# Gaps of 160 and 224 bytes between the weight tiles in on-chip memory

## The chip, the cores and the metric

One core of one Trainium2 chip runs the whole kernel. The metric is the device time of one execution in microseconds (us); the time before is the median of three runs.

## The reference

Eight sequences of 3,072 vectors of 256 floats pass through three layers, all in float32:

```python
X = np.fft.fft(np.fft.fft(x, axis=1), axis=2).real        # 8 x 3072 x 256
x = X.reshape(24576, 256)
# mixture of 8 experts, the best one only
logits = normalised(x) @ normalised(expert_emb).T / tau
e = argmax(logits); gate = softmax(logits)[e]
x = gate * (relu(x @ w1[e]) @ w2[e])                       # w1: 256x1024, w2: 1024x256
# dense layer
h = x @ w_in                                               # 256x2048
out = maximum(0.01 * h, h) @ w_out                         # 2048x256
```

## The kernel before

**Layers.** `batch` computes the two Fourier transforms of one sequence as matmuls with small tables (`smat`, lines 339 to 345, and `cols`, line 453), writes the rows to memory and lets `route` choose each token's expert and write its number into that expert's list. `main` then works through pages of 256 tokens of one expert. A page's rows are gathered, turned by TensorE (`split_t`, line 931) and passed through the expert (`m1_a`, line 947, then `m1_b`, line 965) and the dense layer (`m2_a`, line 1020, then `m2_b`, lines 1056 to 1060). Pages that no expert fills are done in halves by `m3_a` (line 979) and `m3_b` (line 992).

**Precision.** Each float32 operand of these layers is held as a sum of a high and a low part, and a product is made of three matmuls: high by high, high by low, low by high (`PASS`). Both operands have the type float32r.

**A matmul's two operands.** TensorE first loads the stationary operand, 128 columns, and then streams the other one through. In the profile the first is LDWEIGHTS (PEld) and the second MATMUL (PE). In `m1_a`, `m1_b` and `m2_a` the weights `w1`, `w2` and `wi` are stationary and the tokens `xt`, `hh` and `yt` are streamed, 256 columns at a time. In `m2_b` it is the other way: the tokens `hh` are stationary and the weights `wo` are streamed, 512 columns (line 1059, both parts of the weights) and then 256 (line 1060). In `m3_a` and `m3_b`, too, the weights are streamed. Every matmul has a load of its own.

**Memory.** Tiles lie one behind the other in each partition, pool by pool, in the order in which they are first made. The pool `cp` (tables and constants) is first, then `xp`, which begins with the four weight tiles, and last `mp`, which holds `xt`, `yt` and `hh`. `mp` takes the place of `ip`, a pool of the start. The tiles of `mp` are 4,096 bytes a partition each, and `wi`, `wo`, `w1` and `w2` are 32,768, 32,768, 16,384 and 16,384 bytes; within all of these a matmul's operand begins at a multiple of 512 bytes from the tile's start. So the place of an operand modulo 256 is that of its tile.

**Order of the work.** A list of steps written out by `main` sets the order on TensorE: each step issues 12 to 24 matmuls of a first layer (`m1_a`, `m2_a`) and, three steps later, those of the second (`m1_b`, `m2_b`), while `side` mixes in the next sequence's Fourier transform.

Of the kernel before, what the change touches and what calls it, by code (L numbers as in the profile page):

```python
# [6 lines left out]
F32 = mybir.dt.float32  # L7
# [25 lines left out]
BIG = 1e9  # L33
NTB = 3
C3 = 0.8660254037844386
LAG = 3
AHEAD = 13
GAP = 1
# [25 lines left out]
class K:  # L64
# [9 lines left out]
    def run(self):  # L74
        nc, V, a, tc = self.nc, self.V, self.a, self.tc
        dram = self.pool("dram", 1, bass.MemoryType.DRAM)
        self.xd = dram.tile([NTOK, D], F32, name="xd")
        self.tables = [dram.tile([E * NTOK + T, 4], F32, name=f"table{i}") for i in range(NTB)]
        self.bigd = dram.tile([128, 768], F32, name="bigd")
        self.yd = dram.tile([REST + T, D], F32, name="yd")  # L80
        self.dt = dram.tile([REST + T, 4], F32, name="dt")
        self.leftd = dram.tile([NB * 8, 2, 6, 16], F32, name="leftd")
        cp = self.pool("cp", 1)
        self.psm = self.pool("psm", 1, bass.MemoryType.PSUM)
        self.xp = self.pool("xp", 1)
        self.wi = self.xp.tile([128, 2, 2, F2], F32R, name="wi")
        self.wo = self.xp.tile([128, 2, 16, D], F32R, name="wo")
        self.w1 = self.xp.tile([128, 2, 2, F1], F32R, name="w1")
        self.w2 = self.xp.tile([128, 2, 8, D], F32R, name="w2")
        self.wide, self.turn = True, 0  # L90
        with tc.manual_schedule():
            self.consts(cp)
            self.main()

    def ps(self, tag, shape, bufs):
        return self.psm.tile(shape, F32, tag=tag, name=tag, bufs=bufs)
# [132 lines left out]
    def column_end(self, ip):  # L229
# [10 lines left out]
        for d0, n, s0 in ((4, 2, 0), (8, 2, 2)):  # L240
            V.scalar_tensor_tensor(zp[:, d0:d0 + n], zy[:, 10 + s0:10 + s0 + n], -C3, zy[:, 5 + s0:5 + s0 + n], op0=ALU.mult, op1=ALU.add)
            yield
        for d0, n, s0 in ((6, 1, 4), (7, 1, 1), (10, 2, 2)):
            V.scalar_tensor_tensor(zp[:, d0:d0 + n], zy[:, 10 + s0:10 + s0 + n], C3, zy[:, 5 + s0:5 + s0 + n], op0=ALU.mult, op1=ALU.add)
            yield
# [102 lines left out]
    def s_stage(self, j, f, gd, z, left, ptmp):  # L348
# [13 lines left out]
        for par, (sa, sb) in enumerate(r1):  # L362
# [7 lines left out]
            o = 513 + 512 * par  # L370
            V.scalar_tensor_tensor(z[:, o:o + 256], p[:, l:l + 256], -C3 if j == 0 else C3, tmp[:, l:l + 256], op0=ALU.mult, op1=ALU.add)
            if par == 0:
                pv, tv = (x[:, 0:258].rearrange("p (a b) -> p a b", a=2)[:, :, 0:128] for x in (p, tmp))
                V.scalar_tensor_tensor(z[:, 769:1025].rearrange("p (a b) -> p a b", a=2), pv, C3, tv, op0=ALU.mult, op1=op)
            else:
                V.scalar_tensor_tensor(z[:, 1281:1537], p[:, 0:256], C3, tmp[:, 0:256], op0=ALU.mult, op1=op)
            yield "s"
# [386 lines left out]
    def decodes(self):  # L764
# [41 lines left out]
        def rolling(i, end):  # L806

            run = [unit(i)]
            i += 1
            n = 0  # L810
            while run:
                for g in list(run):
                    if next(g, "end") == "end":
                        run.remove(g)
                        if i < end:
                            run.append(unit(i))
                            i += 1
                            next(run[-1])
                    yield
                    n += 1  # L820
                    if n == SKEW and i < end:
                        run.append(unit(i))
                        i += 1
# [11 lines left out]
    def main(self):  # L835
# [53 lines left out]
        def load_page(u):  # L889
            n = 2 if u < NFULL else 1  # L890
            off = nc.sync.value_load(self.rg[:, 0, u:u + 1], min_val=0, max_val=ZPAGE * 2 // n)
            t3 = self.xp.tile([128, NTB, 8], F32, tag="t3", name="t3", bufs=2)
            for i, tb in enumerate(self.tables):
                nc.sync.dma_start(out=t3[:, i, 0:4 * n], in_=tb[bass.ds(off * (H * n), H * n)].rearrange("(p h) w -> p (h w)", h=n))
            t3s[u] = t3[:, :, 0:4 * n]
# [45 lines left out]
        def m1_a(u, s, fill):  # L941
            p = self.ps("h", [128, 2, T], 3)
            xt = xts[u]
            for f in range(2):
                fc = 2 * s + f
                for k, (dc, (wa, xa)) in enumerate([(dc, ps_) for dc in range(2) for ps_ in PASS]):
                    nc.tensor.matmul(p[:, f], self.w1[:, wa, dc, fc * 128:(fc + 1) * 128], xt[:, xa, dc], start=(k == 0), stop=(k == 5))  # L947
            h = self.mp.tile([128, 2, 2, T], F32R, tag="hh", name="hh", bufs=LAG + 1)
            nc.scalar.activation(h[:, 0], p, AF.Relu)  # L949
# [78 lines left out]
        def split_g():  # L1028

            if owed:  # L1030
                m, u, s, g = owed.pop()
                h = self.mp.tile([128, 2, 2, T], F32R, tag="hh", name="hh", bufs=LAG + 1)
                if m == 3:
# [44 lines left out]
        def at(i, fn, *args):  # L1078
            hooks.setdefault(max(0, i), []).append((fn, args))
# [4 lines left out]
        for n, (i, u) in enumerate(firsts):  # L1084
# [5 lines left out]
            if n:  # L1090
# [4 lines left out]
                s0, s1 = end, min(end + 1, i)  # L1095
                s2, s3 = max(pos[pm, pu, na // 2 - 1] + LAG + 2, s0 + 2), max(min(end + LAG, i + LAG), s1 + 2)
                at(max(ip_ + 1, ls[0]), wload, u, 0)
# [10 lines left out]
        for t in range(NTF):  # L1108
            i = [k for k, s in enumerate(steps) if s == (2, NU + t, 0)][0]
# [11 lines left out]
        with tc.tile_pool(name="ip", bufs=1) as self.ip:  # L1121
# [34 lines left out]
            fetch_page(0)  # L1156
            load_page(1)
        self.mp = self.pool("mp", 1)
        self.wide = False
        for _ in range(FIRST[2]):  # L1160
            next(dec)
# [36 lines left out]
        def lag(n):  # L1198

            return 1 if steps[n] in ((1, 0, 3), (1, 1, 3)) else LAG if n > SHORT else 2  # L1200

        done = 0
        for i in range(len(steps) + LAG):
            for fn, args in hooks.get(i, ()):
# [161 lines left out]
```

## Time and profile before

| | |
|---|---|
| three runs | 3680.07, 3681.48, 3687.99 us; median 3681.48 us |
| the profiled execution | 3645.73 us, its span 3644.0 us |
| TensorE, mean granted clock | 0.985 |
| matmuls (MATMUL records) | 26,433 |
| TensorE busy / loading | 97% / 92% of the span |
| VectorE, ScalarE, GpSimd busy | 66%, 53%, 18% |

The span runs from the first to the last instruction of the profiled execution, and 1.7 us of that execution lie outside it. The busy share of TensorE says how long a matmul was under way, not how fast the columns ran: matmuls overlap, so the time of a stretch comes from the distance between their starts.

### The profile page before, as it was taken

How to read it: one execution, taken by the hardware profiler on the slowest of the kernel's cores; microseconds unless marked ns; L12 is line 12 of the kernel's file. 1: busy time of each engine (PE TensorE's matmuls, PEld its weight loads, DVE VectorE, ACT ScalarE, POOL GpSimd, SP SyncE). 2: the span in 40 equal slices, each digit the busy share in tenths (PEclk: the TensorE clock that was granted, in tenths of full speed). 3: DMA queues.
4: the chain of work that ended last, by engine and by line, in shares of the span. 5: the costliest groups of instructions: out<-in, count | busy, mean ns of one | idle time of the engine just before them, and what ended most of it. 6: DMA issues, size and time to landing. Idle time of an engine off the chain costs nothing. (4 is left out here: it accounts for less than half of the span.)

```text
span 3644.0 us, 69226 instructions
## 1 busy us (share of the span) xinstructions
PE 3517.8 (97%) x26433; PEld 3352.5 (92%) x26433; DVE 2413.9 (66%) x4783; ACT 1919.5 (53%) x3475; POOL 671.2 (18%) x620
## 2 busy tenths in 40 slices
PE   4598999999999999999999999999999999999998
PEld 3588999999999999999999999999999999999998
DVE  8776766666666766667666675667676567777654
ACT  3354446554655446554565446554555456666543
POOL 2214111411122111411114111231114111111100
PEclk8799999999999999999999999999999999999999
DMA  4432323332323322332233323232233245555300
GB/s 159 138 122 91 103 65 104 87 133 64 109 71 113 97 72 95 86 116 82 80 99 89 124 71 95 87 104 92 80 100 88 76 124 159 152 154 153 103 24 15
DMA packets 266145, 362.22 MB, mean 99 GB/s; under 512 B 75984, under 2 KB 216659, under 8 KB 265620
## 3 DMA queue, kind: packets, MB, share of 16 engines
q1 hardware_dynamic: 238896, 303.66, 27.6%
q0 software_dynamic: 25184, 52.35, 4.4%
q8 instruction: 207, 3.39, 0.4%
q10 hardware_dynamic: 1732, 1.79, 0.2%
q14 instruction: 126, 1.03, 0.1%
HBM read 304.64 MB, written 63.41 MB: 101 GB/s over the span
## 5 line engine op out<-in xcount | busy, mean ns | idle before, releaser
L1020 PE MATMUL h<-yt,wi 128*128 128x256 f32 x9216 | 1216.6, 281 | 1.1 <-DVE yt L970 1.1
L1020 PEld LDWEIGHTS h<-yt,wi 128*128 128x128 f32 x9216 | 1135.8, 189 | 14.5 <-DVE yt L970 1.3
L1059 PE MATMUL o<-wo,hh 128*128 128x512 f32 x3008 | 1104.1, 400 | 6.9 <-DVE ob L1070 6.9
L1022 ACT ACTIVATE g<-h 128x512 f32<-128x512 f32 x768 | 457.4, 596 | 788.0 <-PE h L1020 782.6
L1060 PE MATMUL o<-wo,hh 128*128 128x256 f32 x3008 | 844.5, 281 | 0.0
L1023 DVE TENSOR_TENSOR g<-g,h 128x512 f32<-128x512 f32 x768 | 525.5, 684 | 451.7 <-ACT g L1022 449.1
L1059 PEld LDWEIGHTS o<-wo,hh 128*128 128x128 f32 x3008 | 566.1, 188 | 109.6 <-DVE ob L1070 7.1
L925 DVE TENSOR_TENSOR w<-raw,w 128x1024 fp32r<-128x1024 f32 x440 | 536.7, 1223 | 148.6 <-ACT w L924 145.6
L1071 POOL DMA_INDIRECT out<-ob,tab x192 | 208.4, 1085 | 2268.6 <-DVE ob L1070 1982.3
L1060 PEld LDWEIGHTS o<-wo,hh 128*128 128x128 f32 x3008 | 568.7, 189 | 1.6
L965 PE MATMUL y<-hh,w 128*128 128x256 f32 x4272 | 566.1, 282 | 1.9 <-DVE w L925 1.3
L947 PE MATMUL h<-xt,w 128*128 128x256 f32 x4224 | 557.4, 282 | 4.6 <-ACT xt L933 3.6
L950 DVE SCALAR_TENSOR_TENSOR hh<-h,hh 128x512 fp32r<-128x512 f32 x356 | 245.9, 691 | 453.9 <-ACT hh L949 453.9
L947 PEld LDWEIGHTS h<-xt,w 128*128 128x128 f32 x4224 | 524.5, 190 | 19.6 <-ACT xt L933 4.3
L965 PEld LDWEIGHTS y<-hh,w 128*128 128x128 f32 x4272 | 528.7, 189 | 3.0 <-DVE w L925 1.5
L1040 DVE TENSOR_TENSOR hh<-g,hh 128x512 fp32r<-128x512 f32 x768 | 525.7, 684 | 1.5 <-ACT hh L1039 1.4
L924 ACT ACTIVATE w<-raw 128x1024 fp32r<-128x1024 f32 x440 | 462.2, 1055 | 94.1 <-DMA raw<-w 93.2
L949 ACT ACTIVATE hh<-h 128x512 fp32r<-128x512 f32 x356 | 213.0, 598 | 551.9 <-PE h L947 550.7
L1039 ACT ACTIVATE hh<-g 128x512 fp32r<-128x512 f32 x768 | 479.0, 624 | 13.1 <-DVE g L1023 12.5
L902 POOL DMA_INDIRECT xr<-xd,tab x199 | 247.3, 1243 | 501.6 <-issue 295.3
L608 POOL DMA_INDIRECT table<-tb,sli x192 | 208.3, 1085 | 192.2 <-DVE tb L602 58.1
L931 PE MATMUL a<-ident,xr 128*128 128x128 f32 x426 | 66.0, 274 | 43.0 <-DMA xr<-xd,tab 43.0
(301 smaller groups left out, 2050.2 us busy)
## 6 DMA issues: line engine op xcount, KB each, us to landing
raw<-w SPq DMA_DIRECT2D x440, 512.0 KB
x<-xl SPq DMA_DIRECT2D x32, 768.0 KB
xd<-xo SPq DMA_DIRECT2D x96, 256.0 KB
table<-bigd SPq DMA_DIRECT2D x21, 384.0 KB
t<-table SPq DMA_DIRECT2D x267, 4.0 KB
xr<-xd,tab POOLq DMA_INDIRECT x199, 4.8
table<-tb,sli POOLq DMA_INDIRECT x192, 3.3
rawz<-w_out SPq DMA_DIRECT2D x6, 512.0 KB
```

The source lines that it names most:

```text
L902: nc.gpsimd.indirect_dma_start(out=self.xr[seq[u] % NX][:, h], out_offset=None, in_=self.xd[0:rows, :], in_offset=bass.IndirectOffsetOnAxi ...
L924: nc.scalar.activation(hi, r, AF.Copy)
L925: V.tensor_tensor(lo, r, hi.bitcast(F32), op=ALU.subtract)
L947: nc.tensor.matmul(p[:, f], self.w1[:, wa, dc, fc * 128:(fc + 1) * 128], xt[:, xa, dc], start=(k == 0), stop=(k == 5))
L965: nc.tensor.matmul(y[:, x], self.w2[:, wa, fc, xs_], h[:, ha, f], **st)
L1020: nc.tensor.matmul(p[:, f], self.wi[:, wa, dc, fc * 128:(fc + 1) * 128], yt[:, xa, dc], start=(k == 0), stop=(k == 5))
L1022: nc.scalar.activation(g, p, AF.Copy, scale=0.01)
L1023: V.tensor_tensor(g, g, p, op=ALU.max)
L1039: nc.scalar.activation(h[:, 0], g, AF.Copy)
L1040: V.tensor_tensor(h[:, 1], g, h[:, 0].bitcast(F32), op=ALU.subtract)
L1059: nc.tensor.matmul(o[th], h[:, 0, f, tk], self.wo[:, :, fc], start=(fc == 0), stop=False, skip_group_check=True)
L1060: nc.tensor.matmul(o[th][:, 0], h[:, 1, f, tk], self.wo[:, 0, fc], start=False, stop=(fc == 15), skip_group_check=True)
```

## The change

Five entries `GAPS` in bytes, and a helper that takes a tile of that size from a pool and never uses it. A gap of 224 bytes is put ahead of `wi`, one of 160 ahead of `wo`, none ahead of `w1`, one of 224 ahead of `w2`, and one of 160 at the head of `mp`.

```diff
+GAPS = 224, 160, 0, 224, 160
...
         self.xp = self.pool("xp", 1)
+        self.hole(self.xp, 0)
         self.wi = self.xp.tile([128, 2, 2, F2], F32R, name="wi")
+        self.hole(self.xp, 1)
         self.wo = self.xp.tile([128, 2, 16, D], F32R, name="wo")
+        self.hole(self.xp, 2)
         self.w1 = self.xp.tile([128, 2, 2, F1], F32R, name="w1")
+        self.hole(self.xp, 3)
         self.w2 = self.xp.tile([128, 2, 8, D], F32R, name="w2")
...
+    def hole(self, pool, i):
+
+        if GAPS[i]:
+            pool.tile([128, GAPS[i] // 4], F32, name=f"hole{i}")
...
         self.mp = self.pool("mp", 1)
+        self.hole(self.mp, 4)
```

`wi` moves by 224 bytes, `wo` and `w1` by 384, `w2` and all later tiles of `xp` by 608, and the tiles of `mp` by 768, which is three times 256. In words of the change, the streamed operand's address less the stationary one's becomes 160 (`m1_a`), 192 (`m1_b`) and 64 (`m2_a`) modulo 256, and 96 in `m2_b`. No instruction is added, removed or moved.

## Rows read from the trace of the kernel before

**Rows 1.** The page: span, and TensorE's busy time, share, instructions.

```profile
span 3644.0 us, 69226 instructions
...
PE 3517.8 (97%) x26433; PEld 3352.5 (92%) x26433; DVE 2413.9 (66%) x4783; ACT 1919.5 (53%) x3475; POOL 671.2 (18%) x620
```

**Rows 2.** Windows, core 0: two of seven stretches, us and (instructions).

```profile
core 0: us, PE busy (x) PEld busy (x) DVE busy (x) ACT busy (x) POOL busy (x), PEclk, DMA share, GB/s
...
0.00:141.00 141.00, 51.51 (x280) 47.13 (x280) 106.38 (x376) 47.41 (x120) 39.81 (x65) 0.73 0.47 152
...
1000.00:2000.00 1000.00, 1000.00 (x7631) 956.90 (x7631) 658.03 (x1285) 527.79 (x947) 207.95 (x184) 1.00 0.30 92
```

**Rows 3.** Waits of TensorE, 400 to 3600 us: all there are.

```profile
PE a L585 <- DVE ohb L577: 1.2, 1, 1.2
```

**Rows 4.** Groups by line, TensorE, whole span: count, busy us, mean ns.

```profile
L1020 PE MATMUL h<-yt,wi 128*128 128x256 f32 x9216 | 1216.6, 281 | 1.1 <-DVE yt L970 1.1
L1059 PE MATMUL o<-wo,hh 128*128 128x512 f32 x3008 | 1104.1, 400 | 6.9 <-DVE ob L1070 6.9
L1060 PE MATMUL o<-wo,hh 128*128 128x256 f32 x3008 | 844.5, 281 | 0.0
L965 PE MATMUL y<-hh,w 128*128 128x256 f32 x4272 | 566.1, 282 | 1.9 <-DVE w L925 1.3 <-ACT w L924 0.6
L947 PE MATMUL h<-xt,w 128*128 128x256 f32 x4224 | 557.4, 282 | 4.6 <-ACT xt L933 3.6 <-DVE xt L934 0.8
```

**Rows 5.** Timeline of TensorE from 2004.6 us: start, length, count.

```profile
2004.69 0.40 PE L1059 MATMUL o<-wo,hh 128*128 128x512 f32 x1
2004.92 0.28 PE L1060 MATMUL o<-wo,hh 128*128 128x256 f32 x1
...
2006.09 1.57 PE L947 MATMUL h<-xt,w 128*128 128x256 f32 x12
2007.50 0.39 PE L1059 MATMUL o<-wo,hh 128*128 128x512 f32 x1
```

**Rows 6.** Timeline of TensorE from 329 us, in a stretch at half clock.

```profile
333.98 0.63 PE L1059 MATMUL o<-wo,hh 128*128 128x512 f32 x1
...
335.89 2.34 PE L1020 MATMUL h<-yt,wi 128*128 128x256 f32 x10
```

**Rows 7.** Windows: that stretch, with the granted clock (PEclk).

```profile
329.00:338.50 9.50, 5.33 (x21) 4.95 (x22) 3.67 (x9) 0.63 (x1) 3.36 (x3) 0.50 0.59 196
```

**Rows 8.** Timeline from 2002.5 us, TensorE and its loads.

```profile
2002.81 0.28 PE L1060 MATMUL o<-wo,hh 128*128 128x256 f32 x1
2002.81 0.19 PEld L1059 LDWEIGHTS o<-wo,hh 128*128 128x128 f32 x1
```

**Rows 9.** Timeline from 173.0 us: a matmul behind which no load follows.

```profile
173.98 0.40 PE L1056 MATMUL o<-wo,hh 128*128 128x256 f32 x2
...
174.92 1.25 PEld L1056 LDWEIGHTS o<-wo,hh 128*128 128x128 f32 x10 [0.75 <-DVE hh L1040]
```

**Rows 10.** Groups in windows of 0.08 us, each holding one such matmul.

```profile
L1056 PE MATMUL o<-wo,hh 128*128 128x256 f32 x1 | 0.3, 280 | 0.0
...
L1056 PE MATMUL o<-wo,hh 128*128 128x256 f32 x1 | 0.3, 282 | 0.0
...
L1056 PE MATMUL o<-wo,hh 128*128 128x256 f32 x1 | 0.3, 277 | 0.0
```

**Rows 11.** By tile, 400 to 3600 us: duration ns minimum/median/maximum.

```profile
L1020 PE MATMUL h<-yt,wi x8523: 273/280/370, 399.8 to 3599.4; 128*128 128x256 f32 x199
...
L1059 PE MATMUL o<-wo,hh x2842: 389/393/586, 400.2 to 3599.8; 128*128 128x512 f32 x190
L1060 PE MATMUL o<-wo,hh x2841: 275/281/287, 400.4 to 3599.7; 128*128 128x256 f32 x190
```

**Rows 12.** Groups in windows of 0.025 us at 1993.9 and 1856.1 us.

```profile
L1059 PE MATMUL o<-wo,hh 128*128 128x512 f32 x1 | 0.4, 403 | 0.0
...
L1059 PE MATMUL o<-wo,hh 128*128 128x512 f32 x1 | 0.4, 393 | 0.0
```

## The prediction, made before the result was known

> **What bounds the kernel now.** I read the page first, then the windows by stage, the waits of TensorE, its groups by line, and last the timeline, where the distance between starts can be read. On the page TensorE is busy for 97% of the span [rows 1]. The windows say where the other 3% lie: in the first 141 us TensorE is busy for 51.51 us, while from 1000 to 2000 us it is never idle [rows 2]. From 400 to 3600 us it waits once, for 1.2 us [rows 3]. So no engine, queue or transfer sets the time of these 3,200 us; only how fast matmul follows matmul does. Anything that makes one matmul in this stream a nanosecond longer or shorter is paid at once, some 20,700 times for those of 256 columns (9,216 + 3,008 + 4,272 + 4,224) and 3,008 times for those of 512 [rows 4]. The other 2,705 of the 26,433 records, a tenth of them [rows 1], I leave out.
>
> The timeline gives the rate. Twelve matmuls of line 947 take from 2006.09 to 2007.50 us, 117.5 ns each, and four pairs of lines 1059 and 1060 from 2004.69 to 2006.09 us, 350 ns a pair [rows 5]. [...]
>
> [...]
>
> **The change part by part.** The gaps add no instruction, transfer or wait; the 768 bytes a partition cost nothing in time. What they move is worked out from the tile sizes. `mp` moves by 768 bytes, so `xt`, `yt` and `hh` keep their place modulo 256. `wi` moves by 224, `w1` and `wo` by 384 (128 modulo 256), `w2` by 608 (96). Taking these shifts back out of the change's own numbers gives the relation before: 64 + 224, 160 + 128 and 192 + 96 are all 288, or 32 modulo 256, for `m2_a`, `m1_a` and `m1_b`; and 96 - 128 is -32, or 224, for `m2_b`. So all stages now have the two operands within 32 bytes of each other modulo 256, and the change takes them 64 to 96 bytes apart. The other tiles of `xp` move too: the Fourier stage's operands by 96 modulo 256 and the transfers' targets with them. That costs nothing here: its matmuls are among the tenth left out, and the transfers land under a TensorE that waits 1.2 us in all [rows 3]; if that cover were gone, the wait would be seen on TensorE by line 947 or 965.
>
> Does the relation matter? A load starts at the moment at which the stream before it does: line 1060 streams and line 1059 loads from 2002.81 us on [rows 8]. So both read at once, and a clash between them is possible. [...]
>
> *From below.* Some matmuls of the start are followed by no load, because the next operand isn't ready: the second of the two of line 1056 at 173.98 us has the next load at 174.92 us [rows 9]. Such ones take 280, 282 and 277 ns; the eight that I read have a mean of 280.0, and three of them are shown [rows 10]. The median with a load beside is 280 (line 1020) and 281 (line 1060) [rows 11]. So a load beside costs a 256-column stream 0 to 1 ns, and most of its excess stays when there is nothing to clash with: 1 ns x 20,720 = 21 us at the most.
>
> *From above.* The same matmul of line 1059, the third of its step and with operands in the same tiles, takes 403 ns in one page and 393 in another [rows 12]. Its addresses are the same both times, so I put the difference down to the moment at which stream and load meet. How they meet is worth up to 10 ns of a 512-column stream. The median is 393 [rows 11], so most meet well; if all did badly it would be 10 x 3,008 = 30 us more. The pairs of rows 5 take 350 ns where 393 and 281 would make 347; I take 4 ns for the mean, 12 us.
>
> The widest bounds are the extremes of the groups: 275 and 287 ns against 281, and 389 against 393 [rows 11]. If every matmul reached its group's best, it would be 6 x 20,720 + 4 x 3,008 = 124 + 12 = 136 us less.
>
> [...]
>
> I take 21 + 12 = 33 us off: two operands that start together within 32 bytes modulo 256 are the relation at which they would most often want the same place, and the change leaves it in all four stages. That sign is an argument from the layout; no row shows another relation in these stages, and the rows bound the size alone.
>
> **The sum.** 3645.7 - 33 = 3612.7 us against the profiled execution, which was 35.8 us faster than the median of the runs. None of the steps touches that distance, so it is carried over: 3681.5 - 33 = 3648 us, 0.9% faster. A measurement here can tell 0.2%, some 7 us, from no change.
>
> **The rivals.**
>
> *Nothing happens (25%).* Load and stream do not meet, as the eight lone matmuls say, and the excess is the stream's own. Against it: the two lengths of one matmul. Time: 3681 us, within 0.2%. [...]
>
> *Slower (20%).* The relation sets the phase in which load and stream lock, and the new one is worse. The place is `m2_b`, with its two lengths: every 512-column stream at 403 ns is 30 us more. If the 256-column ones lose 1 ns as well, 21 us: 3681.5 + 51 = 3733 us. It decides from the point at which a 256-column stream's mean rises by 0.4 ns (8 us), since that alone is past 0.2%. For it: the kernel's median is already at the better length of 393, so there is more to lose there than to win.
>
> *Much faster (10%).* The excess is mostly a clash after all, and a matmul nears its group's best: 136 us less, 3545 us. Against it: the lone matmuls. [...]
>
> **How the numbers follow.** The forecast, 3648 us, has 45%; its own range goes from 8 us less, where it ends in no change, to 70 us less, twice the sum: 3611 to 3673 us. Faster: 45 + 10 = 55%; the same: 25%; slower: 20%. The range for 8 in 10 goes down to the middle of what lies between 70 and 136 us less, 103 us, 3578 us, and so leaves out half of the much faster case, 5%. Upwards it goes to 3715 us, two thirds of the way to the slower rival's price, and I leave out some 12% there.
>
> **What the profile after would show.** If the steps are right, waits and counts stay as they are, TensorE is as busy, and the median of lines 947, 965 and 1020 falls by about 1 ns, with the distance between their starts at 116 to 117 ns; the pair of lines 1059 and 1060 comes to 345 or 346 ns, and 403 becomes rare. If nothing happens, all these stay to the nanosecond. If line 1059's median goes to 400 or more, the slower rival is right. The forecast fails if a stage's relation is worse than the present one while others gain, or if the excess was a clash that the lone matmuls hide, for instance one with their own load.

## The result, and the profile after

The changed kernel took 3637.01 us (median of 3 runs, 3635.68 to 3646.85) against 3681.48 us: 44.5 us less, a ratio of 0.9895 with a 95% interval of [0.9874, 0.9917]. Six more runs against 25 of the kernel before gave 3637.3 against 3671.2 us, 0.9908 [0.9891, 0.9924]: 34 us less. This second pair is the better measured.

The two first profiles don't show that gain. Their executions took 3645.73 us before and 3646.85 us after: the one before was 36 us below its kernel's median, the one after the longest of its kernel's three runs. The page after, span and busy times, against [rows 1]:

```profile
span 3645.1 us, 69226 instructions
...
PE 3512.2 (96%) x26433; PEld 3338.5 (92%) x26433; DVE 2413.7 (66%) x4783; ACT 1917.7 (53%) x3475; POOL 690.2 (19%) x620
```

The counts are those of before. The windows after, two stretches, against [rows 2]:

```profile
0.00:141.00 141.00, 52.51 (x280) 47.92 (x280) 106.52 (x376) 47.45 (x120) 40.31 (x65) 0.73 0.47 152
1000.00:2000.00 1000.00, 1000.00 (x7669) 955.35 (x7669) 660.81 (x1289) 528.50 (x951) 216.73 (x184) 1.00 0.30 92
```

In the same 1000 us, never idle in either kernel, TensorE now begins 7669 matmuls instead of 7631, 0.5% more. Over the 3,200 us from 400 to 3600 that would be 0.5% x 3200 = 16 us, a first estimate of the gain in the streams' rate; the count over the same matmuls below gives 13. Where it lies is seen in the durations by tile after, 400 to 3600 us (minimum/median/maximum ns), against [rows 11]:

```profile
L1030 PE MATMUL h<-yt,wi x8531: 276/278/562, 399.8 to 3600.0; 128*128 128x256 f32 x199
L957 PE MATMUL h<-xt,w x3936: 277/281/287, 404.5 to 3417.4; 128*128 128x256 f32 x197
L975 PE MATMUL y<-hh,w x3936: 276/276/470, 414.4 to 3427.3; 128*128 128x256 f32 x197
...
L1069 PE MATMUL o<-wo,hh x2844: 388/394/628, 400.3 to 3598.5; 128*128 128x512 f32 x190
L1070 PE MATMUL o<-wo,hh x2844: 275/279/415, 400.5 to 3598.7; 128*128 128x256 f32 x190
```

Line numbers are ten higher. The two lines of before that [rows 11] leave out:

```profile
L947 PE MATMUL h<-xt,w x3936: 273/281/288, 401.6 to 3415.2; 128*128 128x256 f32 x197
L965 PE MATMUL y<-hh,w x3936: 275/280/469, 411.4 to 3425.3; 128*128 128x256 f32 x197
```

Line 975 (`w2`) lost 4 ns of its median and line 1030 (`wi`) 2; line 957 (`w1`) stands still, and the 512-column line 1069 has 1 ns more. The timeline after shows the rate by the starts, as [rows 5] do:

```profile
2016.64 1.52 PE L975 MATMUL y<-hh,w 128*128 128x256 f32 x12
2018.00 1.52 PE L1030 MATMUL h<-yt,wi 128*128 128x256 f32 x12
2019.36 1.52 PE L975 MATMUL y<-hh,w 128*128 128x256 f32 x12
2020.72 1.52 PE L1030 MATMUL h<-yt,wi 128*128 128x256 f32 x12
2022.08 0.40 PE L1069 MATMUL o<-wo,hh 128*128 128x512 f32 x1
...
2023.49 0.75 PE L1030 MATMUL h<-yt,wi 128*128 128x256 f32 x5
```

The same two lines in turn, in the kernel before:

```profile
2015.93 1.56 PE L965 MATMUL y<-hh,w 128*128 128x256 f32 x12
2017.33 1.56 PE L1020 MATMUL h<-yt,wi 128*128 128x256 f32 x12
2018.73 1.45 PE L965 MATMUL y<-hh,w 128*128 128x256 f32 x11
```

Twelve matmuls of lines 975 and 1030 take 1.36 us here, 113.3 ns each, where before took 1.40 us, 116.7 ns; not all steps of these lines are so quick, as the experiments show. The four pairs of lines 1069 and 1070 take 1.41 us, 352.5 ns a pair, where before took 350. The waits after, 400 to 3600 us, against the single row of [rows 3]:

```profile
PE h L1030 <- issue: 4.5, 6, 1.0
PE a L595 <- DVE ohb L587: 1.5, 1, 1.5
PE o L1070 <- issue: 0.7, 1, 0.7
PE h L1030 <- remote: 0.4, 1, 0.4
PE o L1069 <- issue: 0.4, 1, 0.4
```

"Issue" means that TensorE waited for nothing that the profile shows and yet began no matmul. Before's first profile has none of it. So the two first profiles hide the gain: a quicker stream here, and stalls of a kind that the execution before happened not to have.

### The profile page after: what moved, and what is told of

The parts are those of the page before. It is cut to its first block, busy times and chain, and to the rows that moved or that the text cites. A ratio compares the mean times of both kernels' runs of the same rounds, so it can differ in the third digit from the quotient of the medians.

```text
span 3645.1 us, 69226 instructions
## 1 busy us (share of the span) xinstructions
PE 3512.2 (96%) x26433; PEld 3338.5 (92%) x26433; DVE 2413.7 (66%) x4783; ACT 1917.7 (53%) x3475; POOL 690.2 (19%) x620
## 5 line engine op out<-in xcount | busy, mean ns | idle before, releaser
L975 PE MATMUL y<-hh,w 128*128 128x256 f32 x4272 | 555.7, 279 | 2.0 <-DVE w L935 1.3
L975 PEld LDWEIGHTS y<-hh,w 128*128 128x128 f32 x4272 | 518.9, 189 | 3.0 <-DVE w L935 1.5
L912 POOL DMA_INDIRECT xr<-xd,tab x199 | 258.4, 1299 | 508.2 <-issue 297.7
```

The source lines that it names most:

```text
L912: nc.gpsimd.indirect_dma_start(out=self.xr[seq[u] % NX][:, h], out_offset=None, in_=self.xd[0:rows, :], in_offset=bass.IndirectOffsetOnAxi ...
L975: nc.tensor.matmul(y[:, x], self.w2[:, wa, fc, xs_], h[:, ha, f], **st)
```

## The experiments

A short name for what is varied: the relation of a stage is its streamed less its stationary address modulo 256. Taking it modulo 256 is the change's own choice: in d3_wo and d2_m1 the tokens move by 256 and 512 bytes against `wi`, and the mean distance of that stage's starts is 118.3 and 118.5 ns where c0_before has 118.6. The kernel before has 32 for `wi`, `w1` and `w2` and 224 for `wo`; the changed kernel has 64, 160, 192 and 96. Two experiments run the kernels as they are, two leave out transfers, and all others change only the list `GAPS` of the changed kernel.

**Both kernels again**, without an edit.

> The kernel before, unchanged, beside itself. If the 44 us between the medians come from the change, this gives 3680 us again and a profile of 3680 us, whose stretches would show where the 35 us lie that the first profiled execution (3645.7 us) lacked. If they come from the execution (some executions of one kernel near 3646 us, some near 3681 us), this kernel's times spread over both.

> The changed kernel, unchanged. Theory of the relation: the starts of lines 1030 and 975 stay 114 ns apart in the median (117 before), which is worth 13 us from 400 to 3600 us in the two traces, so the ratio to before is 0.996 to 0.997 when both run on one chip in turn. If the 44 us are the change's, the ratio is 0.988 to 0.990.

The kernel before gave 3671.62 us, 0.9998 [0.9984, 1.0013]; the changed one 3637.3 us, 0.9908. This time the profiled executions are typical: 3669.6 and 3637.1 us. The waits of TensorE, 400 to 3600 us, kernel before:

```profile
PE h L1020 <- issue: 5.7, 11, 0.8
PE o L1059 <- issue: 4.0, 7, 0.9
PE a L585 <- DVE ohb L577: 1.2, 1, 1.2
...
```

and changed kernel:

```profile
PE a L595 <- DVE ohb L587: 1.5, 1, 1.5
PE o L1070 <- issue: 0.2, 1, 0.2
```

The timeline of the kernel before, second profile, shows what these stalls look like and what GpSimd does meanwhile:

```profile
683.69 0.98 POOL L608 DMA_INDIRECT table<-tb,sli  x1 [0.30 <-issue]
...
684.49 0.35 PE L1020 MATMUL h<-yt,wi 128*128 128x256 f32 x1 [0.28 <-issue]
...
684.97 0.98 POOL L608 DMA_INDIRECT table<-tb,sli  x1 [0.30 <-issue]
...
685.92 0.40 PE L1059 MATMUL o<-wo,hh 128*128 128x512 f32 x1 [0.72 <-issue]
...
686.63 0.39 PE L1059 MATMUL o<-wo,hh 128*128 128x512 f32 x1 [0.20 <-issue]
687.34 0.38 PE L1060 MATMUL o<-wo,hh 128*128 128x256 f32 x1 [0.31 <-issue]
688.05 0.39 PE L1059 MATMUL o<-wo,hh 128*128 128x512 f32 x1 [0.34 <-issue]
```

The slowest of these matmuls come 0.71 us apart instead of 0.12 to 0.23, while line 608 issues its indirect transfers one behind the other. The load on the DMA engines is not the reason, as the window of this stall shows (its last three numbers: granted clock, busy share of the DMA engines, GB/s):

```profile
684.00:690.00 6.00, 3.66 (x18) 2.42 (x17) 2.49 (x3) 2.66 (x4) 4.78 (x5) 1.00 0.03 2
```

In the other four stalls of this trace, too, the DMA engines are busy for 3 to 4% at 2 to 3 GB/s. Next, four stretches of 30 us, the same in both kernels, with the count of matmuls in the first brackets of a row and the granted clock behind the last ones. Kernel before, second profile:

```profile
670.00:700.00 30.00, 26.90 (x178) 24.52 (x177) 15.73 (x23) 12.87 (x20) 17.77 (x17) 0.89 0.33 89
1110.00:1140.00 30.00, 28.70 (x212) 27.14 (x212) 16.30 (x25) 13.84 (x24) 14.40 (x13) 1.00 0.35 82
1540.00:1570.00 30.00, 28.02 (x201) 26.07 (x201) 15.64 (x24) 12.90 (x22) 12.77 (x13) 1.00 0.30 64
1970.00:2000.00 30.00, 27.10 (x184) 25.02 (x184) 14.04 (x21) 12.06 (x20) 11.57 (x12) 0.94 0.22 62
```

Changed kernel, second profile:

```profile
670.00:700.00 30.00, 30.00 (x234) 28.76 (x233) 18.44 (x29) 15.73 (x25) 18.41 (x17) 1.00 0.34 90
1110.00:1140.00 30.00, 30.00 (x235) 28.84 (x234) 16.07 (x26) 13.46 (x23) 14.69 (x14) 1.00 0.37 87
1540.00:1570.00 30.00, 30.00 (x232) 28.76 (x231) 18.17 (x28) 15.39 (x25) 10.14 (x10) 1.00 0.46 110
1970.00:2000.00 30.00, 30.00 (x232) 28.71 (x231) 18.41 (x29) 15.98 (x26) 8.12 (x8) 1.00 0.44 117
```

Matmuls: 178 + 212 + 201 + 184 = 775 against 933. At the changed kernel's 120 / 933 us each, the 158 missing ones are some 20 us (roughly, since the mix of lines differs). In the first and the last of these stretches the granted clock also stood below full speed, at 0.89 and 0.94 on the mean: after 13 matmuls in the 4 us from 686 us it stood at 0.54 in the next 4 us, and after 11 in the 4 us from 1,976 us at 0.57, so partly near the 0.50 of [rows 7]. Part of what a stall costs is the slower clock: at 0.50 a pair of lines 1059 and 1060 took 637 ns [rows 6, 7], at 1.00 it took 350 [rows 5].

So the 34 us have two parts. The table gives both for every kernel. Rates are the mean distance in ns from one start to the next, 400 to 3600 us, distances of 320 ns and more left out; "pair" is a 512- and a 256-column matmul of the output weights; "stalled" is what steps took beyond the median of like steps, summed from 400 us on over those that exceed it by more than 6% plus 60 ns. Some 8 us of it are in every kernel, the stall-free ones too. All kernels issue the same matmuls in the same order, so "stretch" times the same 24,180 of them in each profile, those from 400 to 3600 us in the first profile of before. A ratio is to the kernel before run beside it.

| kernel | relation wi, w1, w2, wo | wi | w1 | w2 | pair | stalled us | stretch us | median us | ratio |
|---|---|---|---|---|---|---|---|---|---|
| before, first profile | 32, 32, 32, 224 | 118.3 | 117.5 | 118.0 | 352.5 | 7.9 | 3200.0 | 3681.48 | |
| c0_before | 32, 32, 32, 224 | 118.6 | 117.5 | 118.0 | 352.9 | 29.1 | 3221.1 | 3671.62 | 0.9998 |
| c1_after | 64, 160, 192, 96 | 116.7 | 118.2 | 115.9 | 354.2 | 9.3 | 3187.1 | 3637.3 | 0.9908 |
| c2_all96 | 32, 32, 32, 224 | 118.7 | 117.6 | 118.7 | 352.8 | 25.1 | 3222.9 | 3672.59 | 1.0012 |
| c3_mp96 | 128 in all | 120.1 | 118.6 | 119.8 | 351.3 | 19.3 | 3232.8 | 3685.58 | 1.0045 |
| d4_zero | 0 in all | 120.9 | 119.8 | 121.2 | 354.6 | 16.7 | 3259.5 | 3711.86 | 1.0125 |
| d1_wi | 64, 32, 32, 224 | 119.1 | 117.5 | 118.5 | 353.6 | 28.5 | 3228.0 | 3672.97 | 1.0005 |
| d2_m1 | 32, 160, 192, 224 | 118.5 | 117.6 | 115.1 | 354.3 | 31.6 | 3213.9 | 3661.79 | 0.9976 |
| d3_wo | 32, 32, 32, 96 | 118.3 | 117.1 | 117.9 | 353.7 | 33.1 | 3224.7 | 3670.96 | 1.0013 |
| e3_wi_w2 | 64, 32, 192, 224 | 117.3 | 117.6 | 115.4 | 352.6 | 15.4 | 3189.4 | 3631.58 | 0.9907 |
| f1_192 | 192, 192, 192, 224 | 115.6 | 114.5 | 115.1 | 354.7 | 8.4 | 3159.5 | 3604.44 | 0.9879 |

From c0 to c1 the stretch falls by 3221.1 - 3187.1 = 34 us, what the runs gave. The first profile of before, free of stalls, lies between: 21 us are stalls (3221.1 to 3200.0), 13 us the rates (3200.0 to 3187.1). By line these 13 us are 13.8 (`wi`) + 8.0 (`w2`) - 2.7 (`w1`) - 7.1 (pairs) + 0.9 (all others). The 13 us are what the first theory on c1_after had foreseen; the stalls it left out. In every kernel of the table nearly all that is stalled beyond the common 8 us lies where line 608 (618) issues.

**Addresses moved, relations kept.** All weights and streamed tiles move by 96 bytes together.

```
-GAPS = 224, 160, 0, 224, 160
+GAPS = 96, 0, 0, 0, 0
```

> Weights and tokens all moved by 96 bytes, their relations as before (32, 32, 32 and 224). Theory of the relation: median distance of starts 117 ns in lines 1030, 957 and 975 and the time of before within 0.2%. Theory of the place (what counts is where weights or streams lie, not how they stand to each other): distances differ from before by 1 ns or more.

3672.59 us, 1.0012 [0.9999, 1.0025]. Moving all operands alike changes the time by nothing that can be told from noise. In the trace it isn't quite nothing: `w2` went from 118.0 to 118.7 ns, since most of its steps take 117.8 instead of 116.7. The relation moves a stage by up to 6 ns, so it is what counts most, but the place has a small say that no run explains.

**The farthest and the nearest relation.**

```
-GAPS = 224, 160, 0, 224, 160
+GAPS = 0, 0, 0, 0, 96      (c3_mp96: 128 in all)
+GAPS = 0, 0, 0, 0, 224     (d4_zero: 0 in all)
```

> Only the tokens moved, by 96 bytes: the streamed less the stationary address is 128 in all four stages, the farthest apart modulo 256. Theory of the relation as I put it (close is bad, far is good): lines 1030 and 975 at 114 ns or less, and line 957 as well, 0.3 to 0.9% faster than before. Theory that each stage has a relation of its own that suits it: some stages get faster and others slower, sum within 0.3%. Theory of the place of the weights: as before.

> Streamed and stationary address at one place modulo 256 in all four stages (relation 0), only the tokens moved. The prediction's reason (close together clashes most) wants this to be the slowest of all: 118 ns or more in lines 957, 975 and 1030 and slower than before by 0.3% or more. The rival, that each stage answers in its own way and closeness means nothing, leaves it open, within 1% of before on either side.

3685.58 us, 1.0045 [1.0029, 1.0061] and 3711.86 us, 1.0125 [1.0101, 1.0148]: both slower than before, without a change in the work. The durations by tile at relation 0, 400 to 3600 us:

```profile
L1030 PE MATMUL h<-yt,wi x8280: 274/283/383, 400.3 to 3599.3; 128*128 128x256 f32 x198
L957 PE MATMUL h<-xt,w x3936: 278/283/287, 403.2 to 3473.7; 128*128 128x256 f32 x197
```

With 283 ns where 280 and 281 stood, relation 0 is the worst that was run, as closeness would have it; but 128, as far apart as two addresses can be modulo 256, is worse than 32: 118.6 to 120.1 ns in the three stages (c3_mp96) against 117.5 to 118.6 (c0_before). Distance is not the rule.

**One part of the change alone.**

```
-GAPS = 224, 160, 0, 224, 160
+GAPS = 224, 32, 0, 0, 0        (d1_wi: wi at 64)
+GAPS = 0, 0, 128, 224, 160     (d2_m1: w1 at 160, w2 at 192)
+GAPS = 0, 128, 128, 0, 0       (d3_wo: wo at 96)
```

> Only the relation of the dense layer's first half (wi) as in the change, 64; the others as before. By the traces of before and after the starts of line 1030 come 1.6 ns closer in the mean, 13 to 14 us from 400 to 3600 us. Theory that the gain is the sum of the stages' rates: 0.4% faster than before and no more. Theory that most of the 34 us is fewer stalls of instruction issue, which come or stay away by a shift in time: the rate gives 14 us, and the rest of the ratio may go either way, between 1.000 and 0.990.

> Only the expert's relations as in the change (w1 160, w2 192); the dense layer's as before. By the traces line 975 gains 8 us and line 957 loses 2.7. Sum of rates: 5 us, 0.14% faster. Theory of the issue stalls: ratio between 1.000 and 0.990.

> Only the dense layer's second half as in the change (wo 96); the others as before. By the traces the pairs of lines 1069 and 1070 take 2 ns longer, 5 us: sum of rates 0.14% slower. If it comes out faster, the stalls of issue, not the rate, make the difference.

They gave 1.0005 [0.9991, 1.002], 0.9976 [0.996, 0.9993] and 1.0013 [0.9999, 1.0027]: 0.06% together, where the whole gives 0.92%. The parts don't add up, for two reasons. All three keep the stalls (28.5 to 33.1 us), and with them more than half of what the whole gained. And `wi` at 64 is no quicker on its own, as the timeline of d1_wi shows:

```profile
2004.40 1.56 PE L975 MATMUL y<-hh,w 128*128 128x256 f32 x12
2005.80 1.57 PE L1030 MATMUL h<-yt,wi 128*128 128x256 f32 x12
2007.21 1.57 PE L975 MATMUL y<-hh,w 128*128 128x256 f32 x12
```

A step of line 1030 takes 1.41 us, 117.5 ns a matmul, behind a `w2` step at 32; the same line at the same relation takes 113.3 ns behind a `w2` step at 192 in the changed kernel. In 219 of 307 `wi` steps behind `w2` the rate was 113 to 114 ns there, and in 288 of 307 it was near 117.8 here. So a stage at 64 can run at either rate, and which one depends on the step ahead of it. It can reach back further: `w2` at 192 behind `w1` at 160 took 118.0 ns in the changed kernel and 113.7 in d2_m1, which differ only in `wi` and `wo`. Not every relation takes up a quick rate: in d2_m1 `wi` at 32 stayed at 116.4 behind quick `w2` steps. That it is the phase between streams and loads that is handed on is a reading; no run shows it.

**The indirect transfers left out.** These kernels leave out the transfers of line 608 (618), and with them the table that they fill, by which the gathers of line 902 and the stores of line 1071 go. Those two are still issued but move next to nothing, as the software queue shows (packets, MB), before and without the transfers:

```profile
q0 software_dynamic: 25184, 52.35, 4.6%
```

```profile
q0 software_dynamic: 19040, 1.81, 0.4%
```

```
-            nc.gpsimd.indirect_dma_start(
-                out=self.tables[i % NTB][:, :], out_offset=bass.IndirectOffsetOnAxis(ap=sli[:, i:i + 1], axis=0),
-                in_=tb[:, i], in_offset=None, bounds_check=E * NTOK - 1, oob_is_err=False)
```

> The kernel before without the indirect transfers of line 608, so that no token is entered in an expert's list and the gathers and the last stores move nothing; the matmuls are all there. Theory that the 34 us are two things, 10 us of a faster stream and some 20 us of stalls of instruction issue that fall in the stretches of these transfers: the stalls go, and this comes out 20 to 30 us under before, near 3645 us, with a TensorE that waits for issue under 1 us. Theory that the stalls are spread by chance and have nothing to do with these transfers: TensorE still waits for issue.

> The changed kernel without the same transfers. Two things: it is 8 to 15 us (0.2 to 0.4%) faster than the kernel before without them, near 3635 us, and no longer 34 us. If the whole 34 us are the stream's rate, the distance to the kernel before without them stays 30 us or more.

Before without them: 3627.31 us, 0.9888 [0.9872, 0.9903]. After without them: 3608.21 us, 0.9844 [0.983, 0.9857]. In neither profile is there a wait for issue (stalled: 7.6 and 8.5 us), and the rates stay: all of the kernel before's within 0.3 ns of its first profile, all of the changed kernel's within 0.4. The kernel before lost 41 us, more than the 20 to 30 expected, because only half of it is stalls: the stretch fell from 3221.1 to 3199.7 us, and the start, up to the stretch, from 402.8 to 380.3. In the changed kernel, which has no stalls to lose, the stretch stayed (3187.1 and 3186.5 us) and the start fell by 30 us. Without the transfers the change is worth 19 us, more than the 8 to 15 expected: 13 in the stretch, as with the transfers, and 6 in the start. The windows of the two, before and after, agree with the rate alone:

```profile
1000.00:2000.00 1000.00, 1000.00 (x7622) 956.72 (x7621) 652.72 (x1268) 522.86 (x942) 134.93 (x114) 1.00 0.25 75
```

```profile
1000.00:2000.00 1000.00, 1000.00 (x7662) 955.43 (x7661) 656.57 (x1262) 527.29 (x948) 138.46 (x115) 1.00 0.26 79
```

40 matmuls more, as between the first two profiles (38). The stream's gain doesn't need the indirect transfers. The stalls seem to: they lie where line 608 issues, and no longer occur without it. One profile of each is little for this, as before's first profile was free of stalls with the transfers in place, and the gathers and stores are emptied along with them. And the transfers alone aren't enough, since the changed kernel has them all.

**The two quick stages alone**, `w1` and `wo` back at the relations of before.

```
-GAPS = 224, 160, 0, 224, 160
+GAPS = 224, 32, 0, 352, 160
```

> Relations of wi and w2 as in the change (64 and 192), those of w1 and wo as before (32 and 224). Theory that a step hands the next the moment at which load and stream lock: behind fast steps of line 975 (113 to 114 ns) line 1030 has 113 ns in many steps, as in the changed kernel and unlike the run with wi alone, and its mean is 116.7 ns or less; line 957 is back at 117.5 ns and a pair at 350 ns, so the stream's rate is 5 to 8 us better than the changed kernel's. If the stages were independent, line 1030 would be at 119 ns as in the run with wi alone. The time: 3625 to 3632 us if the stalls of issue stay away as in the changed kernel, 3645 to 3655 us if they come as in the others.

3631.58 us, 0.9907 [0.9891, 0.9922], the changed kernel's ratio. Against d1_wi only `w2` has another relation, and `wi` behind it is quick now: 113 to 114 ns in 269 of 307 steps, where d1_wi has 18. This is the plainest case of a rate that depends on the step ahead. The mean of `wi`, 117.3 ns, misses the 116.7 that was expected, because of its steps behind the output weights: 1 of 287 is at 113 to 114 ns here (`wo` at 224), 160 of 286 in the changed kernel (`wo` at 96). The pair is back at 352.6 ns, and some 6 us of stalls are left between 2,766 and 2,806 us. So the parts of the change at `w1` and `wo` earn nothing in sum: `wo` at 96 makes its own matmuls slower and the `wi` steps behind them quicker.

**192 everywhere.** `w2` at 192 was quick behind quick and slow `wi` steps alike, so the last run puts `wi` and `w1` there too, and `wo` back at 224.

```
-GAPS = 224, 160, 0, 224, 160
+GAPS = 96, 160, 96, 0, 160
```

> All three stages that stream 256 columns are put at the relation 192, the output weights of the dense layer stay at 224 as in the kernel before. Theory 1, each relation has its own rate, whatever the stage: the stage with w2 ran at 113.3 to 113.8 ns a matmul at 192 in two kernels, so the stages with wi and w1 come to the same. Against the changed kernel that is 2.9 ns x 9,216 for wi (116.7 to 113.8), 4.4 ns x 4,224 for w1 (118.2 to 113.8), about 2 ns x 4,272 for w2 and 1.7 ns x 3,008 for the pair of the output weights: 27 + 19 + 8 + 5 = 59 us, so about 3575 to 3590 us, 2.2 to 2.6 per cent faster than before, and faster than the changed kernel. Theory 2, the rate is handed from step to step and 192 was quick only for w2 behind its neighbours: wi stays between 116 and 119 ns and w1 near 117.6, and the time is 3620 to 3665 us. A rate of 119 ns or more at wi or w1, with a time of 3690 us or more, would say that the good relation differs by stage.

3604.44 us against 3646.32 us for the kernel before on the same chip, 0.9879 [0.9863, 0.9896]: 42 us less. The windows and the durations by tile:

```profile
1000.00:2000.00 1000.00, 1000.00 (x7747) 955.61 (x7746) 661.13 (x1291) 531.47 (x955) 214.58 (x188) 1.00 0.30 91
```

```profile
L1030 PE MATMUL h<-yt,wi x8640: 276/276/367, 411.9 to 3585.9; 128*128 128x256 f32 x197
L957 PE MATMUL h<-xt,w x3936: 276/276/384, 400.8 to 3375.6; 128*128 128x256 f32 x197
L975 PE MATMUL y<-hh,w x3936: 276/276/470, 410.5 to 3385.6; 128*128 128x256 f32 x197
```

All three stages have a median of 276 ns, and 116 matmuls more than before start in the 1000 us. Theory 1 came nearer than theory 2, but neither gave the time: 3604 us lies above the one's 3575 to 3590 and below the other's 3620 to 3665. The mean over all steps, 114.5 to 115.6 ns, is above the 113.3 to 113.8 that theory 1 took from the best ones, and the pair did not come back to 352.5 ns: it takes 354.7, though `wo` stands at 224 as before, so here, too, a relation has no fixed rate. The profiled run is 33 us shorter than the changed kernel's, 28 of them in the stretch, where theory 1 had 59. As a ratio the gain is smaller still, because the kernel before was itself 25 us quicker here than in the other comparisons. 3646.3 us is what its first profile took, the one without stalls (3645.7 us), and its seven runs here, up to 3651.3 us, all lie below the fastest run of the other comparisons (3655.4). That this chip spared it the stalls is argued from these times; no trace of the kernel before was taken there. What the rates are worth doesn't hang on it: against the stall-free first profile of before the stretch is 3200.0 - 3159.5 = 40.5 us shorter in this version and 13 us in the change.

## Why the prediction was right, and where not

**What bounds the kernel: right.** Nothing else came into play in the stream: same counts, and a rate that changed at once with nothing but addresses (the stretch took 3222.9 us in c2_all96, 3232.8 in c3_mp96 and 3259.5 in d4_zero).

**That the relation matters: right.** If load and stream did not meet, as the rival of no change has it, all relations would give one time. Here the same 24,180 matmuls take from 3159.5 us (192 in three stages) to 3259.5 us (0 in all, 9 us of it stalls), so the measurement decides against that rival for this pair of operands.

**That closeness is what hurts: wrong.** Relation 0 is the slowest, but 128 is slower than 32, and the quick ones are 192 and, behind a quick step, 64. The sign was right for the change as a whole, and for two of its four stages. `w1` and `wo` became slower while `wi` and `w2` gained, which the prediction had itself named as a way in which it fails (`w1` only in company: with `wo` left at 224, in d2_m1, it took 117.6 ns at 160). What makes a relation quick stays open: six were run in the stages that stream 256 columns, and no run shows what in the memory or in TensorE tells them apart.

**The price of a 256-column matmul, 1 ns x 20,720 = 21 us: the bound failed.** The "excess" that it bounds is what a matmul takes beyond the passing of its columns, and no run shows what the columns alone need; an estimate from [rows 6, 7], half of the 637 ns that a pair took at a clock of 0.50, is some 318 ns, against the 350 of [rows 5]. The bound itself came from lone matmuls with no load behind them. Lines 975 and 1030 gained 3.4 ns a matmul in their quick steps behind one another (116.7 to 113.3), line 957 nothing. In the stretch the three lines make 13.8 + 8.0 - 2.7 = 19.1 us together; that this comes close to the predicted figure is chance. A lone matmul's duration was the wrong row: it says how long the record is (277 to 282 ns [rows 10]), not how close the next start can follow (116.7 ns in lines 965 and 1020).

**The 512-column matmuls, 4 ns x 3,008 = 12 us: wrong in sign.** The pair went from 352.5 to 354.2 ns, the median of line 1059 from 393 to 394, and the stretch shows 7 us more for the pairs. This was the place and the sign of the slower rival, at a quarter of its 30 us.

**The 35.8 us between profile and median, carried over: wrong.** Between the first two profiles of before, 24 us apart, 21 us are stalls of issue during the indirect transfers, which the first didn't have; the other 12 us up to the median of 3681.5 us no trace shows. The step "none of the steps touches that distance" failed: a profile of the changed kernel as quick as its median (c1_after) has nearly none of them, and over half of the measured gain is there. So 3648 us forecast and 3637 us measured lie only 11 us apart because two errors work against each other: a stream gain of 13 us instead of 33, and stalls that weren't foreseen, 21 us in the traces and 31 if the rest of the 44.5 is theirs. That the time came out as near as it did is luck.

**What stays open.** Why the stalls stay away in the changed kernel and in e3_wi_w2 (but for one stretch from some 2,770 to 2,820 us, 12 us of it in the first profile after) while d1, d2 and d3 have them in full. With it stays open the cause of 21 of the 34 us. Moving the tiles alike doesn't do it (c2_all96: 25.1 us). The kernels that are free of them are those with the quickest streams, which fits a matter of when the transfers meet the stream, but no run separates the two; before's first profile was free of them at the slower rate, and by the last comparison the chip may have a say as well.

## What to carry to other kernels

When TensorE is never idle, take its rate from the distance between starts, by step, and try the offset between streamed and stationary tiles in steps of 32 or 64 bytes modulo 256: it costs a few hundred bytes and moved this kernel's matmuls by some 3% between worst and best (3259.5 and 3159.5 us for the stretch, 9 us of it stalls). Change it for all stages that follow each other at once, since one stage alone may stay at its neighbour's slower rate, as `wi` at 64 did in d1_wi (119.1 ns). And where the profiled execution is far from the median, find what differs between the two before any gain is added to either.

## What the runs showed of the hardware

- Matmuls of 256 columns with a new load each gather, step by step, at a few distances, among them 113.3 to 114 ns (c1_after, e3_wi_w2), 116.7 and 117.8 (the kernel before) and 120.0 (relation 0, d4_zero). At a granted clock of 0.50 a pair, 768 columns, took 637 ns [rows 6, 7]; at twice that rate, which is an estimate from these rows alone, 256 columns would need 106, and the quickest step of twelve in the first profile after took 113.3 a matmul.
- The rate belongs to the relation and to what ran ahead: `wi` at 64 ran at 113 to 114 ns behind `w2` at 192 in 269 of 307 steps (e3_wi_w2) and near 117.8 behind `w2` at 32 in 288 of 307 (d1_wi).
- While GpSimd issued indirect transfers back to back, TensorE began matmuls as much as 0.71 us apart for stretches of a few us, some 20 us in a run, with the DMA engines busy for 3 to 4% (c0_before); without those transfers neither profile has it (7.6 and 8.5 us stalled, e1_before_noscat and e2_after_noscat), and with them not every one does. One and the same kernel has executions with and without: 7.9 us stalled in one of 3645.7 us (the first profile of before), 29.1 us in one of 3669.6 (c0_before).
